# Linear attention with an FFN on one core: the row maxima of K as bias of the exponentials, v in bf16 and unscaled, a new order of the work

## The chip, the cores and the metric

The kernel runs on one core of one Trainium2 chip. Its time is that of one execution on the device, in microseconds (us). Five engines work side by side, each through its own instructions in order: TensorE (PE, the matrix products, with a separate row for loading its weights, PEld), VectorE (DVE), ScalarE (ACT), GpSimd (POOL) and SyncE (SP). PE writes its products into eight banks of 128 x 512 floats; DVE and ACT read the banks. DMAs are issued by SP, by POOL (those that convert a type on the way) or by ACT.

## The reference

Eight batches of eight heads, 576 rows of 64 numbers, go through a linear attention with exponential features; the heads are joined and go through a gated FFN of width 1536.

```python
def phi(x):
    proj = np.einsum('bhsd,df->bhsf', x, w_phi)             # 64 -> 128
    proj = proj - np.max(np.abs(proj), axis=-1, keepdims=True)
    return np.concatenate([np.exp(proj), np.exp(-proj)], axis=-1)
q_p, k_p = (phi(q), phi(k))
kv = np.einsum('bhsf,bhsd->bhfd', k_p, v)
z = np.sum(k_p, axis=2)
num = np.einsum('bhsf,bhfd->bhsd', q_p, kv)
den = np.einsum('bhsf,bhf->bhs', q_p, z)[..., None] + 1e-06
x = num / den                                             # then (b s) (h d)
out = (np.maximum(x @ w_gate, 0) * (x @ w_val)) @ w_out
```

With m the row maximum of |proj|, the two halves of a row's features are exp(proj) e^-m and exp(-proj) e^m.

## The kernel before, in words

**Order.** The text ORDER at the top of the file is the program: each word names a step, its indices and, behind the colon, the banks it uses. The last loop of the file calls the steps in that order, and each engine, POOL's and SP's queues of DMAs among them, gets its instructions in this order. No scheduler changes it. A step waits only for the data and the buffers that it needs.

**Tiling.** Of the 576 rows of a batch the first 512 are four tiles of 128; the last 64 of two batches are joined to tiles of a ninth group, "mix". The eight heads are in three groups (`HEADS`: 0-1, 2-4, 5-7; index j). Index i is one of the four tiles.

**K side.** `lk` loads and converts k (POOL). `kt` (DVE), or in batch 0 `k0` and `k1` (PE and DVE), transposes it; `kr` (L476), in batch 0 `k2` (L514), projects it, rows on the partitions, three heads of 128 features in one bank. `ke` (L523) takes exp(proj) and exp(-proj), index s, of 384 columns at a time, and `kx` (L531) the row maxima of |proj|. The factors e^-m and e^m are not put on the features: `kk` (L540) and `kp` (L551) take them as small exponentials of 12 columns, and `vs`, `vo` and `vr` on POOL (L578, L590, L597), in batch 0 also `vd` and `vp` on DVE, multiply v by them, into two scaled copies of v with a column of the factors. `kv` (L618) then adds up five products for each head and sign: four tiles and the joined rest. `kc` or `kd` copies the sums from the bank on ACT or DVE.

**Q side.** `lq` loads q, `qt` transposes it (L645), `qc` and `qs` project it (L654), features on the partitions; `qe` (L669) takes both exponentials of 512 columns, `qx`, `qy`, `qz`, `qu` find the row maxima, `qw` the factor e^2m. `nu` (L717) multiplies with kv, `nt` and `nv` (L738, L748) join the two signs, `nr` and `nx` (POOL, L760) or `ny` (DVE) divide. `xt` (L777) transposes the result x by a DMA on SP's queue; two tiles of batch 0 go by PE instead (`xp`, L782) and a copy by DVE (`xc`, L790).

**FFN.** For batch 0, `pv` and `pg` (L891) start a third of the width for one tile of 128 rows at a time ("half-FFN" in the prediction stands for the first of these steps); for all else `fv` and `fg` (L865) take 128 of the 1536 columns for 512 rows, `va` (ACT, L880) copies the value half, `ga` (DVE, L883) joins it with the gate. `fo` (L920) multiplies with w_out, `oc` (ACT, L929) copies the result and `od` sends it. `mc` to `mn` are the same as the Q side for the mix group.

**Loads.** v comes in float32: batch 0 by POOL's queue in rows of four, the others by SP's queue (`lv`, `lw`) in rows of 64 floats. k, q, v have one buffer each, so that a batch's load waits for the last reader of the batch before; `gt` is a tiny DMA that keeps the load of batch 1's k behind batch 0's. The weights come by POOL's queue in thirds (`wl`, `wo`). `zz` steps are products of zeros that keep PE's clock up while it waits (L373).

Of the kernel before, what the change touches and what calls it, by code (L numbers as in the profile page):

```python
# [16 lines left out]
ms.0 ms.6 wq ms.2 ms.5 wd ms.4 lk.0.1 ms.3 lq.0.1 lk.0.2 id if zz.22:0 k0.1:0 k1.1:0 zz.5:1  # L17
k2.1:1234 ke.0.1.0.0:1 lk.0.0 lm.0.0 qt.0.1 ke.0.1.2.1:3 lm.0.1 kx.0.1.1:2 zz.3:5 k0.2:5
ke.0.1.2.0:3 kx.0.1.0:1 ke.0.1.3.1:4 k1.2:5 ke.0.1.0.1:1 zz.4:6 k2.2:6705 kx.0.1.2:3 wp
ke.0.1.1.0:2 k0.0:1 kx.0.1.3:4 ke.0.1.1.1:2 kx.0.2.1:7 ke.0.2.0.0:6 k1.0:1 ke.0.1.3.0:4  # L20
ke.0.2.3.0:5 kx.0.2.0:6 ke.0.2.1.0:7 kx.0.2.2:0 kk.0.1.0 zz.4:3 k2.0:3241 wc ke.0.2.1.1:7
kx.0.0.2:4 ke.0.0.3.1:1 kk.0.1.1 qs.0.1.0:7 ke.0.0.3.0:1 lv.0.1 lq.0.0 ke.0.2.2.1:0 kx.0.2.3:5
kp.0.2.1:5 ke.0.0.2.1:4 lv.0.0 kx.0.0.1:2 kx.0.0.3:1 qe.0.1.0.1:7 ke.0.2.3.1:5 ke.0.2.2.0:0 qt.0.0
qs.0.0.0:1 lm.1.1 qx.0.1.0:7 ke.0.0.2.0:4 kp.0.2.0:5 ke.0.0.1.0:2 gt.0 ke.0.2.0.1:6 lv.0.2 lw.0.0
lw.0.1 wl.1.0 kx.0.0.0:3 lk.1.3 vd.0.2.0:5 vo.1 lv.1.2 qs.0.1.1:0 wl.0.0 qs.0.0.2:4 ke.0.0.1.1:2
vs.0.1.0 qs.0.0.1:6 vs.0.1.1 kk.0.0.1 vr.0.0.1 qe.0.0.0.1:1 vr.0.1.1 vd.0.2.1:5 qe.0.0.0.0:1
qx.0.0.2:4 qx.0.0.0:1 qe.0.1.0.0:7 kk.0.0.0 vr.0.1.0 qe.0.1.1.0:0 qx.0.0.1:6 qs.0.0.3:2
ke.0.0.0.0:3 qs.0.1.3:7 vr.0.0.0 lw.1.1 vp.2:5 qe.0.0.3.1:2 qx.0.1.1:0 ke.0.0.0.1:3 qs.0.1.2:1
qy.0.0:5 qz.0.0:5 qe.0.0.1.1:6 kv.0.2:3 qx.0.0.3:2 kv.0.1:5 qe.0.1.3.0:7 qu.0.0 qe.0.0.1.0:6
qe.0.1.1.1:0 qx.0.1.2:1 kc.0.2:3 qw.0.0 kc.0.1:5 qx.0.1.3:7 wl.0.1 vs.0.0.1 qy.0.1:6 qz.0.1:6  # L30
kt.1.1 nu.0.0.2:0 vs.0.0.0 nt.0.0.2:0 qe.0.1.2.1:1 vo.0 kv.0.0:3 qe.0.1.2.0:1 kc.0.0:3
qe.0.0.3.0:2 qu.0.1 nv.0.0.2:0 qy.0.2:6 qz.0.2:6 qw.0.1 nu.0.0.1:5 nt.0.0.1:5 qe.0.1.3.1:7
qe.0.0.2.1:4 nu.0.1.1:1 nu.0.0.0:0 qu.0.2 qw.0.2 nv.0.0.1:5 qy.0.3:3 qz.0.3:3 nu.0.1.0:6 zz.2:2
kr.1.1:2537 nt.0.0.0:0 lm.1.0 nt.0.1.0:6 qe.0.0.2.0:4 nv.0.0.0:0 nt.0.1.1:1 ke.1.1.2.0:3 lq.1.2
wl.1.1 nu.0.1.2:0 nr.0.0 nu.0.2.2:4 nv.0.1.1:1 ny.0.0 nt.0.1.2:0 ke.1.1.1.0:5 nv.0.1.0:6
ke.1.1.3.0:7 ke.1.1.0.0:2 ke.1.1.1.1:5 lw.1.0 nv.0.1.2:0 zz.2:1 xp.0.0:1 wl.0.2 xc.0.0:1
nt.0.2.2:4 nr.0.1 nx.0.1 ke.1.1.2.1:3 nu.0.2.0:6 nu.0.2.1:0 qu.0.3 qw.0.3 nt.0.2.0:6 ke.1.1.3.1:7
nv.0.2.2:4 nv.0.2.0:6 ke.1.1.0.1:2 nt.0.2.1:0 pg.0.0:1 kx.1.1.1:5 nv.0.2.1:0 kx.1.1.2:3 pv.0.0:4
xp.0.1:6 nr.0.2 nx.0.2 xc.0.1:6 xt.0.2 pv.1.0:5 nu.0.3.0:0 pa.0.0:4 pb.0.0:1 pa.1.0:5 ln.0.1
pv.0.1:3 pa.0.1:3 lv.1.0 qt.1.1 kx.1.1.3:7 pg.0.1:4 nt.0.3.0:0 kx.1.1.0:2 kk.1.1.0 nv.0.3.0:0  # L40
pb.0.1:4 nu.0.3.1:6 qc.1.1:1537 qe.1.1.0.0:1 nu.0.3.2:2 qe.1.1.0.1:1 nt.0.3.1:6 qe.1.1.1.0:5
nt.0.3.2:2 qe.1.1.3.0:7 nv.0.3.1:6 pv.1.1:0 lv.1.3 nv.0.3.2:2 pg.1.1:4 pa.1.1:0 lv.1.1 nr.0.3
qx.1.1.0:1 qe.1.1.2.0:3 ln.0.0 qe.1.1.1.1:5 qx.1.1.3:7 qe.1.1.3.1:7 pg.1.0:6 pv.0.2:2 nx.0.3 ku.1
pa.0.2:2 xt.0.3 qe.1.1.2.1:3 pg.0.2:1 pb.1.0:6 kt.1.0 kr.1.0:0672 ke.1.0.1.0:6 wo.2 qx.1.1.1:5
wl.1.2 ke.1.0.3.1:2 pb.1.1:4 qx.1.1.2:3 ke.1.0.0.0:0 ke.1.0.2.1:7 ms.1 ke.1.0.2.0:7 kx.1.0.1:6
ke.1.0.1.1:6 pv.1.2:5 lm.2.0 lm.2.1 pb.0.2:1 pa.1.2:5 vs.1.1.0 wo.0 ke.1.0.0.1:0 pg.1.2:4
kx.1.0.3:2 ke.1.0.3.0:2 qt.1.0 fv.0.9:3 kk.1.1.1 kx.1.0.0:0 fv.0.8:1 pv.0.3:6 va.0.9:3 pb.1.2:4
qc.1.0:5203 vs.1.1.1 va.0.8:1 pa.0.3:6 kt.1.2 qx.1.0.1:2 kx.1.0.2:7 qe.1.0.3.0:3 qx.1.0.3:3 lk.2.3
wo.1 pv.1.3:4 qe.1.0.0.0:5 qx.1.0.0:5 qe.1.0.1.0:2 kk.1.0.0 vr.1.1.0 vs.1.0.0 vr.1.0.0
qe.1.0.1.1:2 kk.1.0.1 vo.1.0 vs.1.0.1 qe.1.0.3.1:3 pg.0.3:1 pb.0.3:1 vr.1.1.1 qe.1.0.0.1:5  # L50
pg.1.3:6 vr.1.0.1 qx.1.0.2:0 pa.1.3:4 mt.0 lv.2.3 pb.1.3:6 qe.1.0.2.0:0 fv.0.10:7 kr.1.2:2315
kx.1.2.1:3 fg.0.10:4 ke.1.2.3.1:5 kx.1.2.0:2 fv.0.11:6 qe.1.0.2.1:0 qy.1.0:0 va.0.10:7 kx.1.2.2:1
kx.1.2.3:5 ke.1.2.1.0:3 vo.1.1 qz.1.0:0 qu.1.0 va.0.11:6 ga.0.10:4 fg.0.11:7 ga.0.11:7 kk.1.2.1
vs.1.2.1 kk.1.2.0 ke.1.2.0.0:2 ke.1.2.3.0:5 fg.0.8:6 ga.0.8:6 kv.1.0:0 ke.1.2.1.1:3 ke.1.2.0.1:2
vs.1.2.0 ku.2 ke.1.2.2.1:1 mc.0:4537 lv.2.0 me.0.3.0:7 mx.0.1:5 mx.0.2:3 vo.1.2 mx.0.0:4
ke.1.2.2.0:1 kt.2.0 fg.0.9:2 ga.0.9:2 lv.2.1 qw.1.0 me.0.3.1:7 me.0.1.0:5 me.0.2.0:3 kv.1.1:6
ln.1.0 kv.1.2:1 kc.1.0:0 mx.0.3:7 lm.3.1 kt.2.1 lq.2.2 ln.1.1 nu.1.1.0:0 kc.1.1:6 nu.1.0.1:2
me.0.1.1:5 nt.1.0.1:2 lv.2.2 me.0.0.0:4 nu.1.0.0:6 nt.1.0.0:6 nv.1.0.1:2 nv.1.0.0:6 nu.1.1.1:7
# [12 lines left out]
oc.0.3:1 lk.3.3 kk.2.1.1 mn.0.1:5 nt.8.0.1:5 mn.0.2:7 vr.2.1.0 vr.2.1.1 kx.2.2.2:0 ke.2.2.2.1:0
nv.8.0.1:5 kk.2.2.1 vr.2.0.1 ke.2.2.0.1:3 lw.3.0 nt.8.0.2:7 nv.8.0.2:7 lm.4.1 fv.1.0:2 va.1.0:2
# [164 lines left out]
def kernel(  # L237
# [94 lines left out]
    def v_in(b):  # L332
        return v_one() if b == 1 else vn_of(b)
# [646 lines left out]
```

## Time and profile before

| | |
|---|---|
| median of 3 runs | 387.66 us (385.79 to 388.32) |
| the profiled execution: span from the first to the last instruction | 384.0 us |
| PE busy | 365.5 us (95%), 3551 products |
| DVE busy | 275.2 us (72%) |
| ACT busy | 237.0 us (62%) |
| POOL busy | 160.1 us (42%) |
| moved by DMA | 38.29 MB, mean 100 GB/s |

The profiled execution has only its span; what lies around it is taken as the 3.7 us between span and median. In the profile a busy PE is not PE at its peak, since products overlap; how far apart they start tells more. The same holds for ACT: its mean durations contain an overlap with the next instruction. "Granted clock" is the share of full speed that the throttle gave to TensorE.

### The profile page before, as it was taken

The page shows a single profiled execution, that of the slowest core. Times are in us where ns is not written, and L with a number is a line of the kernel's source. Part 1 is how long each engine was busy: PE and PEld are TensorE (multiplying, and loading weights), DVE is VectorE, ACT ScalarE, POOL GpSimd, SP SyncE. Part 2 cuts the span into 40 slices and gives each one's busy share as a digit, 9 for nine tenths or more (in the row PEclk, how much of TensorE's full clock was granted, in tenths as well). Part 3 has the DMA queues.
Part 4 walks back from the last instruction along what each step waited for, and adds up shares of the span by engine and source line. Part 5 has one row for each costly group of instructions (what it writes and reads, how often), then busy time and mean ns, then how long its engine had stood idle before and what let it go on. Part 6 is the DMA issues. An engine that isn't in the chain of part 4 may idle for free.

```text
span 384.0 us, 9108 instructions
## 1 busy us (share of the span) xinstructions
PE 365.5 (95%) x3551; PEld 193.7 (50%) x3551; DVE 275.2 (72%) x651; ACT 237.0 (62%) x566; POOL 160.1 (42%) x179
## 2 busy tenths in 40 slices
PE   7699679999999999999999999999999999999994
PEld 4268646545544554455545544464445544444442
DVE  4979929999997898788957797798667822521320
ACT  2987849788867915985787647964977213321321
POOL 8593729587366423672393025811462120100000
PEclk9869979999999999999999999999999999999998
DMA  8999999995965765677335742552410031000114
GB/s 131 231 167 183 181 179 154 131 127 81 215 54 124 114 106 81 122 116 109 77 88 93 134 83 65 111 102 56 112 55 2 3 82 56 27 15 0 55 63 103
DMA packets 91456, 38.29 MB, mean 100 GB/s; under 512 B 65302, under 2 KB 86550, under 8 KB 91414
## 3 DMA queue, kind: packets, MB, share of 16 engines
q0 software_dynamic: 33904, 15.23, 30.6%
q1 hardware_dynamic: 57510, 22.49, 27.4%
q8 instruction: 28, 0.46, 0.5%
q14 instruction: 14, 0.11, 0.1%
HBM read 37.95 MB, written 9.44 MB: 123 GB/s over the span
## 4 chain that ended last, share of the span: by engine, by line
PE 85%; DVE 6%; DMA 4%; SPq 1%; issue 1%; POOL 1%; ACT 0%; DVEq 0%; POOLq 0%
PE bank L865 45%; PE bank L920 25%; PE bank L618 6%; PE bank L717 3%; DMA xTs<-xu 2%; PE bank L654 2%; PE bank L476 2%; DMA qn<-in_q_dram 2%; DVE mk L531 1%; DVE t L738 1%; DVE u L748 1%; PE bank L891 1%; SPq L424 1%; DVE maxq L677 1%; PE bank L852 1%
## 5 line engine op out<-in xcount | busy, mean ns | idle before, releaser
L880 ACT CAST val<-bank 128x512 bf16<-128x512 f32 x100 | 58.0, 599 | 77.3 <-PE bank L865 56.4
L883 DVE SCALAR_TENSOR_TENSOR h<-bank,val 128x512 bf16<-128x512 f32 x100 | 66.7, 678 | 50.3 <-PE bank L865 37.0
L920 PE MATMUL bank<-wo,h 128*128 128x512 bf16 x432 | 99.0, 379 | 0.0
L523 ACT ACTIVATE kp<-bank 128x384 bf16<-128x384 f32 x192 | 81.9, 517 | 20.1 <-PE bank L476 8.3
L865 PE MATMUL bank<-xTs,wv 128*128 128x512 bf16 x352 | 88.2, 384 | 5.9 <-DMA xTs<-xu 5.7
L760 POOL TENSOR_TENSOR xu<-u,r 128x512 bf16<-128x512 f32 x35 | 36.4, 1043 | 124.4 <-DVE r L756 81.7
L865 PE MATMUL bank<-xTs,wg 128*128 128x512 bf16 x352 | 87.9, 379 | 0.0
L669 ACT ACTIVATE qp<-bank 128x512 bf16<-128x512 f32 x128 | 70.7, 627 | 4.4 <-PE bank L654 3.7
L920 PEld LDWEIGHTS <-h 128*128 128x128 bf16 x432 | 40.8, 98 | 47.7 <-issue 0.9
L865 PEld LDWEIGHTS <-wv 128*128 128x128 bf16 x400 | 37.1, 98 | 47.9 <-issue 9.7
L578 POOL TENSOR_TENSOR vs<-vn,ek 128x780 bf16<-128x780 f32 (+3 forms) x40 | 53.0, 1341 | 18.7 <-ACT ek L540 12.2
L865 PEld LDWEIGHTS <-wg 128*128 128x128 bf16 x400 | 36.6, 98 | 42.0 <-issue 3.3
L677 DVE TRANSPOSE_TENSOR_REDUCE maxq<-bank 128x16 f32<-128x512 f32 x64 | 42.4, 692 | 16.8 <-ACT val L906 7.3
L531 DVE TENSOR_REDUCE mk<-bank 128x3 f32<-128x384 f32 x96 | 49.3, 542 | 7.0 <-ACT kp L523 4.6
L929 ACT COPY ob<-bank 128x512 f32<-128x512 f32 x36 | 21.4, 598 | 29.9 <-PE bank L920 26.6
L748 DVE TENSOR_TENSOR u<-bank,t 128x195 f32<-128x195 f32 (+1 forms) x108 | 34.3, 332 | 2.7
L738 DVE TENSOR_TENSOR t<-bank,cq 128x195 f32<-128x195 f32 (+1 forms) x96 | 30.1, 327 | 3.2 <-PE bank L717 2.1
L717 PEld LDWEIGHTS <-qp 128*128 128x128 bf16 x512 | 23.8, 99 | 11.6 <-issue 0.6
L717 PE MATMUL bank<-kv,qp 128*128 128x65 bf16 x512 | 26.4, 195 | 0.2
L597 POOL TENSOR_TENSOR vr<-vm,ek 64x260 bf16<-64x260 f32 x32 | 19.7, 618 | 16.7 <-issue 9.8
L618 PEld LDWEIGHTS <-kp 128*128 128x128 bf16 x640 | 24.1, 102 | 3.3 <-DVE h L883 0.2
L618 PE MATMUL bank<-vs,kp 128*128 128x65 bf16 x512 | 24.3, 199 | 0.0
(81 smaller groups left out, 317.9 us busy)
## 6 DMA issues: line engine op xcount, KB each, us to landing
out_dram<-ob SPq DMA_DIRECT2D x32, 256.0 KB, 2.2
vn<-in_v_dram SPq DMA_DIRECT2D x24, 256.0 KB, 4.6
kn<-in_k_dram POOLq DMA_DIRECT2D x7, 512.0 KB, 8.4
qn<-in_q_dram POOLq DMA_DIRECT2D x7, 512.0 KB, 6.2
wg<-in_moe_w_gate_dram POOLq DMA_DIRECT2D x3, 512.0 KB, 8.4
wv<-in_moe_w_val_dram POOLq DMA_DIRECT2D x3, 512.0 KB, 8.6
wo<-in_moe_w_out_dram POOLq DMA_DIRECT2D x3, 512.0 KB, 13.3
vm<-in_v_dram SPq DMA_DIRECT2D x16, 64.0 KB, 4.1
```

What stands on the lines that cost most here:

```text
L523: nc.scalar.activation(kp_of(3 * b + j)[:, i, s].rearrange("p n f -> p (n f)"), bank[bk[0]][:, 0 : 3 * F], AF.Exp, scale=(1.0, -1.0)[s],)
L531: nc.vector.tensor_reduce(mk_of(3 * b + j)[:, :, i], bank[bk[0]][:, 0 : 3 * F].rearrange("p (n f) -> p n f", f=F), axis=AX.X, op=ALU.max, ...
L578: nc.gpsimd.tensor_tensor(vs_of(3 * b + j)[:, s, 0:n].rearrange("p n i e -> p (n i) e")[:, :, 0:e], src[:, lo:hi].rearrange("p h i e -> p ...
L618: nc.tensor.matmul(out_ps[:, h - lo, s, :], lhsT=lhsT, rhs=rhs, start=(at == 0), stop=(at == 2 * n * (C + 1) - 1),)
L669: nc.scalar.activation(qp_of(4 * b + i)[:, s, 4 * hq : 4 * hq + 4].rearrange("p h m -> p (h m)"), bank[bk[0]], AF.Exp, scale=(1.0, -1.0)[s],)
L677: nc.vector.tensor_reduce(maxq[:, :, i, 4 * hq : 4 * hq + 4].rearrange("p t h -> p h t"), bank[bk[0]].rearrange("p (h t u) -> p h t u", h= ...
L717: nc.tensor.matmul(bank[bk[0]][:, E * n : E * (n + 1)], lhsT=qp_of(4 * b + i)[:, s, h, :], rhs=kv_of(b)[:, h, s, :],)
L748: nc.vector.tensor_tensor(u_of(serial(b, i))[:, lo:hi], parts(bk, n)[:, :, 0], t_of(3 * serial(b, i) + g)[:, 0:n], op=ALU.add,)
L865: nc.tensor.matmul(bank[bk[0]], lhsT=w[:, dc, P * f : P * f + P], rhs=xT(g)[:, dc, :], start=(dc == 0), stop=(dc == NDC - 1),)
L880: nc.scalar.copy(val_of(NFC * g + f), bank[bk[0]])
L883: nc.vector.scalar_tensor_tensor(h2_of(g, f), bank[bk[0]], 0.0, val_of(NFC * g + f), op0=ALU.max, op1=ALU.mult)
L920: nc.tensor.matmul(bank[bk[0]], lhsT=h2_of(g, f)[:, P * t : P * t + P], rhs=wo_sb[:, f, :], start=(f == 0), stop=(f == NFC - 1),)
```

## The change

- `ke` takes one head, 128 columns, at a time, with m or -m as the bias of the exponential, a value per partition read from memory. `kx` writes m, and `kg` (POOL) or `kh` (DVE) writes -m beside it. So the features are scaled, and `kk`, `kp`, `vs`, `vo`, `vr`, `vd`, `vp` are gone.
- v is converted to bf16 by its DMA and goes into `kv` as it is, with a column of ones. All of its loads are on POOL's queue now, in rows of 64, batch 0 too. `gt` is gone; k, q and v have two buffers.
- All four tiles of batch 0's x are transposed by PE (`xp`), with copies by ACT (`xa`, three) or DVE (`xc`, one).
- 36 of the 100 `va` are `vb`, on DVE; 13 of the 36 `oc` are `oe`, on DVE; 17 of the 24 copies of kv are on ACT, 6 before; 8 of the 36 divisions are on DVE, 1 before.
- The last tile is copied in halves by ACT and DVE (`o1`, `o2`), and sent by two DMAs, on SP's and on ACT's queue.
- ORDER is new throughout. Words now also name the buffers (behind @). It begins with 37 zero products in place of 22; the mix group's FFN comes ahead of the last of batch 7's.

```diff
-ms.0 ms.6 wq ms.2 ms.5 wd ms.4 lk.0.1 ms.3 lq.0.1 lk.0.2 id if zz.22:0 k0.1:0 k1.1:0 zz.5:1
+ms.0 ms.1 ms.3 ms.4 ms.2 ms.6 wq wd lk.0.1 ms.8 id zz.37:0 k0.1:0 k1.1:0@kT0 zz.5:1 k2.1:0123 lk.0.2
 ...
-    vn_of = ring("vn", 1, [P, H, C, E], FP32)
+    vn_of = pair("vn", [P, H, C, EP], BF16)
 ...
     def do_lv(bk, b, i):
         if b == 0:
-            lo, hi = HEADS[i]
-            nc.gpsimd.dma_start(
-                out=v_flat()[:, lo:hi],
-                in_=v[b, lo:hi, 0:SF, :].rearrange("h (p c) d -> p h c d", c=C),
-            )
+            src = v[b, :, 0:SF, :].rearrange("h (p c) d -> p h c d", c=C)[:, :, i, :]
         else:
-            nc.sync.dma_start(
-                out=v_in(b)[:, :, i, 0:D],
-                in_=v[b, :, P * i : P * i + P, :].rearrange("h p d -> p h d"),
-            )
+            src = v[b, :, P * i : P * i + P, :].rearrange("h p d -> p h d")
+        nc.gpsimd.dma_start(out=vn_of(b)[:, :, i, 0:D], in_=src)
 ...
     def do_ke(bk, b, j, i, s):
-        nc.scalar.activation(
-            kp_of(3 * b + j)[:, i, s].rearrange("p n f -> p (n f)"),
-            bank[bk[0]][:, 0 : 3 * F],
-            AF.Exp,
-            scale=(1.0, -1.0)[s],
-        )
+        for n in range(3):
+            nc.scalar.activation(
+                kp_of(3 * b + j)[:, i, s, n],
+                bank[bk[0]][:, F * n : F * (n + 1)],
+                AF.Exp,
+                bias=mk_of(3 * b + j)[:, s, i, n : n + 1],
+                scale=(1.0, -1.0)[s],
+            )
 ...
+    def negate(eng, b, j, i):
+        mk = mk_of(3 * b + j)
+        eng.tensor_scalar(mk[:, 0, i], mk[:, 1, i], -1.0, None, op0=ALU.mult)
 ...
     def do_kv(bk, b, j):
 ...
-                        rhs = vs_of(3 * b + j)[:, s, h - lo, i, :]
+                        rhs = vn_of(b)[:, h, i, 0:E]
 ...
-                        rhs = vr_of(b)[:, s, h // 2, h % 2, :]
+                        rhs = vr_of(b)[:, h // 2, h % 2, :]
 ...
+    def do_xa(bk, b, i):
+        nc.scalar.copy(
 ...
+    def do_vb(bk, g, f):
+        nc.vector.tensor_copy(val_of(NFC * g + f), bank[bk[0]])
 ...
+    def do_o1(bk, g, t):
+        nc.scalar.copy(ob_of(4 * g + t)[:, 0:HD], bank[bk[0]][:, 0:HD])
+    def do_o2(bk, g, t):
+        nc.vector.tensor_copy(ob_of(4 * g + t)[:, HD:DM], bank[bk[0]][:, HD:DM])
+    def do_d1(bk, g, t):
+        r0 = S * g + P * t
+        nc.sync.dma_start(out=out[r0 : r0 + P, 0:HD], in_=ob_of(4 * g + t)[:, 0:HD])
+    def do_d2(bk, g, t):
+        r0 = S * g + P * t
+        nc.scalar.dma_start(out=out[r0 : r0 + P, HD:DM], in_=ob_of(4 * g + t)[:, HD:DM])
```

More of the change, by code (lines that the diff above doesn't have):

```diff
@@ L23 @@
[L23 to L34, printed above, removed]
@@ L356, in do_if, with ones @@
         nc.vector.tensor_copy(identf, ident)
+    def ones(b):
+        for hh in range(2):
+            r = slice(SM * hh, SM * (hh + 1))
+            nc.vector.memset(vr_of(b)[r, :, hh, D : D + 1], 1.0)
     def do_ms(bk, what):
@@ L790, in do_xc @@
         nc.vector.tensor_copy(
+            xT_cols(b, i),
+            bank[bk[0]].bitcast(BF16)[:, 0 : NDC * P].rearrange("p (a b) -> p a b", b=P),
+        )
+    def do_xa(bk, b, i):
+        nc.scalar.copy(
             xT_cols(b, i),
```

577 lines of the change are left out of this document (290 added, 287 removed).

## The prediction

> **What bounds the kernel now.** I read the busy tenths first, then the table by stage, then PE's waits and PE in order of time, and last ACT's bursts.
>
> From the page, the busy tenths of PE and ACT and the granted clock in 40 slices:
>
> ```profile
> PE   7699679999999999999999999999999999999994
> ...
> ACT  2987849788867915985787647964977213321321
> ...
> PEclk9869979999999999999999999999999999999998
> ```
>
> PE is full from the seventh slice to the last but one. The table by stage (us of the stage, busy us and instructions of PE, weight loads, DVE, ACT, POOL, then granted clock, DMA share, GB/s):
>
> ```profile
> 8.00:32.00 24.00, 18.09 (x243) 11.35 (x238) 21.59 (x53) 21.63 (x58) 15.87 (x21) 0.79 1.22 200
> ...
> 44.00:60.00 16.00, 10.34 (x124) 6.36 (x122) 8.66 (x16) 8.96 (x23) 7.94 (x10) 0.79 1.29 181
> 60.00:120.00 60.00, 60.00 (x705) 31.83 (x704) 57.53 (x146) 47.76 (x123) 40.63 (x47) 1.00 0.92 123
> ...
> 300.00:384.00 84.00, 79.12 (x431) 36.60 (x427) 27.20 (x63) 21.21 (x39) 5.18 (x5) 0.98 0.16 46
> ```
>
> After 60 us PE is full at clock 1.00, and its instructions follow each other at one step each (four 128x512 matmuls start 0.86 us apart). So the time is: PE's own work, plus what PE loses in the head, plus the tail. By start-to-start steps PE's work is 344 us: 800 matmuls of L865 and 432 of L920 at 0.216 (266), 256 of L891 at 0.0555 (14), 640 of L618 and 512 of L717 at 0.032 (37), the rest (projections, transposes, L852) 27. The last matmul ends at 379.1, so **35 us are lost** in the head (zero matmuls, waits, clock 0.5); the tail is 4.9 us (copy of the last tile 0.59, then its DMA). The span of 384.0 is 3.7 below the median of the runs, 387.66; I add 3.7 to every span.
>
> The largest single loss, in PE's waits and in PE's instructions in order of time (start, us, what):
>
> ```profile
> PE bank L865 <- DMA xTs<-xu: 5.7, 1, 5.7
> ...
> 43.59 1.06 PE L891 MATMUL bank<-xTs,wg 128*128 128x128 bf16 x16
> 50.31 3.50 PE L865 MATMUL bank<-xTs,wv 128*128 128x512 bf16 x8 [5.66 <-DMA xTs<-xu]
> ```
>
> PE waits for x tiles 2 and 3 of batch 0, which go by a DMA transpose behind a full set of loads, and the eight matmuls that follow take 0.43 each in place of 0.216, at half clock: 5.9 + 1.7 = 7.6 us.
>
> **Part by part.**
>
> *x of batch 0 by TensorE.* Two more tiles of four transposes: 8 x 0.056 = 0.45 us of PE, and copies of 0.40 to 0.48 on ACT or DVE. It takes away the 7.6 us, if nothing else is late there. What is late next is ACT's queue, below.
>
> *128-wide exponentials with a bias.* The costly groups (line, engine, operation, count, busy us, mean ns):
>
> ```profile
> L523 ACT ACTIVATE kp<-bank 128x384 bf16<-128x384 f32 x192 | 81.9, 517 | 20.1 <-PE bank L476 8.3
> L578 POOL TENSOR_TENSOR vs<-vn,ek 128x780 bf16<-128x780 f32 (+3 forms) x40 | 53.0, 1341 | 18.7 <-ACT ek L540 12.2
> L597 POOL TENSOR_TENSOR vr<-vm,ek 64x260 bf16<-64x260 f32 x32 | 19.7, 618 | 16.7 <-issue 9.8
> ```
>
> A mean duration overstates ACT, since instructions overlap. ACT in order of time:
>
> ```profile
> 10.38 2.79 ACT L523 ACTIVATE kp<-bank 128x384 bf16<-128x384 f32 x7 [0.46 <-DVE mk L531]
> 12.99 0.27 ACT L540 ACTIVATE ek<-mk 128x12 f32<-128x12 f32 x1
> 13.09 0.93 ACT L523 ACTIVATE kp<-bank 128x384 bf16<-128x384 f32 x2
> 13.84 0.28 ACT L540 ACTIVATE ek<-mk 128x12 f32<-128x12 f32 x1
> 13.94 0.94 ACT L523 ACTIVATE kp<-bank 128x384 bf16<-128x384 f32 x2
> ...
> 27.93 1.12 ACT L669 ACTIVATE qp<-bank 128x512 bf16<-128x512 f32 x2
> 28.89 0.26 ACT L710 ACTIVATE cq<-mz 128x8 f32<-128x8 f32 x1
> ```
>
> Start to start, a 384-wide exponential takes 0.371 (seven from 10.38 to 12.99), a 512-wide one 0.478, and a 12-wide one that reads SBUF 0.10 (13.84 to 13.94). From the first two: 0.833 ns an element and 0.051 us beside; the 12-wide one has 0.092 beside. So a 128-wide exponential from PSUM costs 0.051 + 0.107 = 0.158 if its bias costs nothing, and 0.158 + 0.092 = 0.25 if fetching the row maximum from SBUF costs as much as that read does. Call it p. No row shows an exponential with a bias from memory. I take **p = 0.17**, near the lower end: function, source and destination are those of the 384-wide row, and in the bursts each start lies 0.11 to 0.29 us ahead of the end before it, room enough for a fetch of 0.09. Both ends stay for the range.
>
> By the Trainium skill (ScalarE: Activation LUTs, What ACT_TABLE_LOAD costs) "each `[128,1]` pointer operand adds ≈ 93 ns", and instructions in a row overlap by about 93 ns; before has immediate biases only, so no run here shows it yet. If the 93 ns also stand between two starts, an exponential would take 0.158 + 0.093 = 0.25, the upper end above, and the sum would be that of the second case below.
>
> 192 x 0.371 = 71 us of ACT become 576p: 98 at 0.17, 144 at 0.25. 48 small exponentials (5 us), 36 copies of the value half and 13 output copies (23) leave ACT, 11 copies of kv (4) come. All ACT: 217 before, 220 after (p = 0.17) or 267. DVE takes 36 copies (about 0.60 each, by L629's 260 and 390 wide, 0.41 and 0.55, less the overlap of 0.08) and 13 output copies: 256 to 289 of some 375. POOL loses 82 us (L578, L597, L590) and gains 48 loads of v at 0.75 and 67 negations at about 0.25 (L590 has 0.29 for 24 columns): 157 to some 125. Over the whole span no engine passes PE; what counts is the order in the head.
>
> *The head, on ACT.* PE begins with 37 zero matmuls in place of 22: these 22 end at 5.7 (0.20 each), 15 more at the later 0.109 reach 7.4, and K's first transposes start there in place of 6.6. The first exponential now also needs its row maximum (0.54): 8.3 + 0.8 + 0.6 = 9.7. Up to the first half-FFN of batch 0 ACT has 78 exponentials and 8.8 us of others in its queue; before had 21.5 us and 2.0 us of idle to that point (31.8). So this step comes at 9.7 + 2.0 + 8.8 + 78p = 33.8 for p = 0.17, with 8.8 us of PE's work done: **25 us lost**. At the first gate step over all four tiles (fg.0.10) 131 exponentials and 21.2 us of others lie ahead: 11.7 + 21.2 + 22.3 = 55.2, less 29.2 of PE's work, 26. From there ACT falls behind PE no more at this p: at kv.3.0 (288 exponentials, 46.6 others, PE 90.4) it would allow 17. DVE, by its rows, has 41.8 us ahead of fg.0.10, after 8.5 of early idle, and 29 small negations at 0.1: 52, so it is nearly as late. I add 2.5 for the small waits between the half-FFN and 60 us, of which before has about 4: **28.5 lost**.
>
> *v as bf16, unscaled.* On the path this spares the wait for POOL's scaling (before, DVE scales one group itself, two times 0.94). Its DMAs leave SP's queue for POOL's. All 36,864 rows of v become packets of 128 bytes; such packets took 32 ns in the trace, the present 256-byte ones 23: the v of batches 0 and 1 takes 18.7 us of all 16 DMA engines in place of 11.3, at a share of about 1.25 some 6 us more, behind which the weights lie. Against it, POOL no longer stands 4.2 us for a marker load and k has two buffers. I let these cancel: wo's last third lands near 63 as now, and PE wants its first third at 37.1 + 28.5 = 65.6. So hidden, by a little; this cover gone costs what the load is late.
>
> *Last tile in halves.* The copy goes from 0.59 to about 0.40 (a 256-wide one has 0.41), with two DMAs side by side: 0.4 us off the tail, bounds 0 and 1.
>
> Sum: PE's work with the transposes 344.7, + 28.5 + 4.5 = 377.7 of span, with 3.7 a time of 381; at p = 0.158 the same steps give 1.5 less. I say **380**.
>
> **Rivals.**
> 1. *The bias is paid between two starts (p = 0.25).* Then ACT's queue is the bound for three batches: lost at kv.3.0 are 11.7 + 46.6 + 72 - 90.4 = 40, at the half-FFN 31. Span 344.7 + 40 + 1.5 of waits + 4.5 = 390.7, time **394.5**, slower. It decides from the p at which these losses equal the present 35: about 0.23. For it speaks that the read of SBUF does stand between starts in the 12-wide row (0.092 against 0.051); against it, the starts ahead of ends. Chance 0.25.
> 2. *The loads hold the head.* If the DMA engines keep a share of 1.0 on small packets in place of 1.25, wo is some 7 us late, the loss is 35 as now: **387**. For it: a DMA share of 1.2 to 1.3 all through the head. The Trainium skill (DMA: Bandwidth & Descriptors, Specifications) wants 512 bytes a transfer for full rate; the trace agrees, 512-byte packets taking 64 ns and 128-byte ones 32. Chance 0.10.
> 3. *Small waits eat it.* A negation on POOL stands behind a normalisation (1.04) or a load's issue (0.75) while ACT, in order, waits for it; or p is 0.20, with 30 + 2.5 lost. Either gives **384 to 386**. Chance 0.10.
> 4. The forecast: 375 to 385, chance 0.55.
>
> **Numbers.** One per cent is about what a measurement of this kernel can tell from no change; its edges are 383.8 and 391.5. Faster by more: 0.47 of the forecast, 0.03 and 0.04 of rivals 2 and 3, 0.54. Within: 0.06, 0.05, 0.04, 0.01: 0.16. Slower: 0.24 of rival 1 and 0.06 of the rest: 0.30. The range runs from 374 (p = 0.158, no small waits) to 395.5, which takes in most of rival 1; beyond it lie p near 0.3 and a part of the best cases. The likeliest case's own range is 375 to 385.
>
> **What would show it.** In the changed profile: the start-to-start of the 128-wide exponentials (0.16 to 0.19, or 0.25); no wait of L865's successor for xTs in batch 0; the half-FFN's first matmul near 34 (40 in rival 1); PE full from about 60 on, with ACT at nine tenths to some 55 us only (to 130 in rival 1); PE waiting for a DMA of wo or v in rival 2; ACT waiting for mk from POOL in rival 3. I am wrong if PE still shows idle slices after 65 us, or if DVE, whose 57.53 of 60 us between 60 and 120 leaves least room, becomes what PE waits for.

## The result, and the profile after

The changed kernel takes **443.31 us** (median of 4, 442.99 to 443.63) where the kernel before takes 386.73 (median of 4, 383.21 to 388.32): a ratio of **1.147**, 95% interval 1.141 to 1.152. Forecast was 380.0, with a range up to 395.5. The profiled execution has a span of 441.9 us, 57.9 more than before.

The busy tenths of PE and ACT and the granted clock in 40 slices, from the page of the changed kernel:

```profile
PE   8468888879888699788987999789878999999996
...
ACT  2989999699887656887798635896698630210110
PEclk9759999999999899999999999999999999999999
```

Before, PE stood at nine from the seventh slice on. Now it shows eights and sevens among them as far as the thirty-first slice, some 340 us: the loss is not in the head alone. The table by stage of the changed kernel (stage, its length, then busy us and instructions of PE, weight loads, DVE, ACT, POOL, granted clock, DMA share, GB/s):

```profile
0.00:60.00 60.00, 43.73 (x561) 30.77 (x563) 41.57 (x109) 49.20 (x157) 34.51 (x57) 0.86 1.05 122
60.00:120.00 60.00, 50.50 (x617) 28.34 (x623) 48.38 (x113) 52.69 (x170) 27.91 (x49) 1.00 0.94 107
120.00:180.00 60.00, 51.28 (x479) 26.21 (x485) 47.20 (x114) 40.23 (x120) 20.97 (x33) 0.97 0.58 70
180.00:240.00 60.00, 50.81 (x484) 25.49 (x490) 47.49 (x109) 49.49 (x156) 21.47 (x34) 1.00 0.89 96
240.00:300.00 60.00, 53.16 (x533) 26.99 (x538) 45.32 (x103) 41.95 (x128) 12.79 (x20) 1.00 0.38 52
300.00:360.00 60.00, 52.73 (x462) 26.29 (x471) 43.48 (x98) 43.34 (x126) 5.24 (x11) 1.00 0.17 42
```

From 60 to 360 us PE is busy 258.5 of 300 us; each stage of 60 loses 7 to 10. Before it was busy 299.8 of 300, and the stage in which it was least full was this one:

```profile
120.00:180.00 60.00, 59.77 (x617) 31.24 (x616) 49.83 (x119) 40.78 (x98) 28.93 (x29) 1.00 0.68 112
```

In those 300 us of the changed kernel ACT is busy 227.7 and DVE 231.9: neither is full, not even the engine for whose exponentials PE waits. The chain that ended last, by engine and by line (L543 is the exponential of K, L855 and L916 the FFN):

```profile
PE 42%; ACT 36%; DVE 15%; issue 4%; DMA 2%; POOL 1%; DVEq 0%; ACTq 0%; POOLq 0%
ACT kp L543 25%; PE bank L855 24%; PE bank L916 8%; ACT qp L635 6%; DVE maxq L643 4%; DVE mk L552 3%; DVE h L876 3%; PE bank L584 2%; PE bank L683 2%; DMA xTs<-xu 2%; PE bank L620 2%; PE bank L490 2%; ACT val L870 2%; PE bank L401 1%; DVE u L714 1%
```

Before, ACT had none of this chain:

```profile
PE 85%; DVE 6%; DMA 4%; SPq 1%; issue 1%; POOL 1%; ACT 0%; DVEq 0%; POOLq 0%
```

And PE's waits in the changed kernel (what waits, for whom, us in total, times, longest):

```profile
PE bank L620 <- ACT kp L543: 6.7, 9, 1.6
PE bank L916 <- ACT kp L543: 6.6, 6, 2.0
PE bank L490 <- ACT kp L543: 4.5, 6, 1.3
PE bank L683 <- ACT kp L543: 3.8, 8, 1.2
PE bank L855 <- ACT kp L543: 3.5, 8, 0.9
...
PE bank L855 <- DMA xTs<-xu: 1.9, 1, 1.9
```

Many waits of about one us, at every kind of product. All rows of this list add up to 53 us, and those that end with an exponential of K to 31 of them; before, all rows were 13 us. The one long wait of before (5.7 us for xTs in batch 0) is gone; the 1.9 us for xTs here come at 239 us, in a later batch.

What an exponential costs is read from ACT in order of time (start, us, what, count, idle before). First the changed kernel, then the experiment n128_no_bias below, which differs only in having no bias. Each row begins with the first exponential of K:

```profile
9.50 6.83 ACT L543 ACTIVATE kp<-bank,mk 128x128 bf16<-128x128 f32 x26 [7.50 <-DVE mk L552]
```

```profile
9.15 7.25 ACT L543 ACTIVATE kp<-bank 128x128 bf16<-128x128 f32 x42 [7.14 <-DVE mk L551]
```

In about the same time 26 and 42 instructions. Start to start it is **0.250 us** with the bias (the median of 518 pairs) and **0.158** without (518 pairs too).

### The profile page after: what moved, and what is told of

It is laid out like the page before. It is cut to its first block, busy times and chain, and to the rows that moved or that the text cites. A ratio compares the mean times of both kernels' runs of the same rounds, so it can differ in the third digit from the quotient of the medians.

```text
span 441.9 us, 9415 instructions
## 1 busy us (share of the span) xinstructions
PE 379.5 (86%) x3526; PEld 199.8 (45%) x3575; DVE 316.0 (72%) x726; ACT 286.7 (65%) x867; POOL 123.9 (28%) x201
## 4 chain that ended last, share of the span: by engine, by line
PE 42%; ACT 36%; DVE 15%; issue 4%; DMA 2%; POOL 1%; DVEq 0%; ACTq 0%; POOLq 0%
ACT kp L543 25%; PE bank L855 24%; PE bank L916 8%; ACT qp L635 6%; DVE maxq L643 4%; DVE mk L552 3%; DVE h L876 3%; PE bank L584 2%; PE bank L683 2%; DMA xTs<-xu 2%; PE bank L620 2%; PE bank L490 2%; ACT val L870 2%; PE bank L401 1%; DVE u L714 1%
## 5 line engine op out<-in xcount | busy, mean ns | idle before, releaser
L543 ACT ACTIVATE kp<-bank,mk 128x128 bf16<-128x128 f32 x576 | 160.4, 500 | 26.7 <-DVE mk L552 19.8
L916 PE MATMUL bank<-wo,h 128*128 128x512 bf16 x418 | 99.7, 379 | 7.9 <-ACT kp L543 6.6
L855 PE MATMUL bank<-xTs,wv 128*128 128x512 bf16 x335 | 87.2, 381 | 9.9 <-ACT kp L543 2.3
L855 PE MATMUL bank<-xTs,wg 128*128 128x512 bf16 x336 | 86.0, 379 | 2.8 <-ACT kp L543 1.2
L635 ACT ACTIVATE qp<-bank 128x512 bf16<-128x512 f32 x128 | 72.6, 675 | 12.0 <-DVE maxq L643 6.8
L870 ACT CAST val<-bank 128x512 bf16<-128x512 f32 x64 | 39.7, 625 | 51.1 <-PE bank L855 32.9
L916 PEld LDWEIGHTS <-h 128*128 128x128 bf16 x432 | 40.6, 98 | 53.8 <-issue 9.0
L855 PEld LDWEIGHTS <-wv 128*128 128x128 bf16 x400 | 37.3, 98 | 51.3 <-issue 14.2
L552 DVE TENSOR_REDUCE mk<-bank 128x3 f32<-128x384 f32 x96 | 49.2, 545 | 14.6 <-PE bank L490 12.1
L739 POOL TENSOR_TENSOR xu<-u,r 128x512 bf16<-128x512 f32 x28 | 29.2, 1043 | 107.8 <-DVE r L735 93.1
L855 PEld LDWEIGHTS <-wg 128*128 128x128 bf16 x400 | 37.0, 98 | 45.0 <-issue 7.8
L562 POOL TENSOR_SCALAR mk<-mk 128x3 f32<-128x3 f32 x67 | 15.3, 234 | 119.0 <-DVE mk L552 106.3
L925 ACT COPY ob<-bank 128x512 f32<-128x512 f32 x22 | 14.6, 663 | 41.8 <-PE bank L916 41.0
L873 DVE CAST val<-bank 128x512 bf16<-128x512 f32 x36 | 24.4, 683 | 13.8 <-PE bank L855 13.5
L683 PE MATMUL bank<-kv,qp 128*128 128x65 bf16 x512 | 28.1, 194 | 5.6 <-ACT kp L543 3.8
L445 POOL DMA_DIRECT2D vn<-in_v_dram x32 | 29.5, 923 | 1.5 <-issue 0.7
```

The costliest lines, as they stand in the source:

```text
L543: nc.scalar.activation(kp_of(3 * b + j)[:, i, s, n], bank[bk[0]][:, F * n : F * (n + 1)], AF.Exp, bias=mk_of(3 * b + j)[:, s, i, n : n + 1 ...
L552: nc.vector.tensor_reduce(mk_of(3 * b + j)[:, 1, i], bank[bk[0]][:, 0 : 3 * F].rearrange("p (n f) -> p n f", f=F), axis=AX.X, op=ALU.max, ...
L635: nc.scalar.activation(qp_of(4 * b + i)[:, s, 4 * hq : 4 * hq + 4].rearrange("p h m -> p (h m)"), bank[bk[0]], AF.Exp, scale=(1.0, -1.0)[s],)
L683: nc.tensor.matmul(bank[bk[0]][:, E * n : E * (n + 1)], lhsT=qp_of(4 * b + i)[:, s, h, :], rhs=kv_of(b)[:, h, s, :],)
L855: nc.tensor.matmul(bank[bk[0]], lhsT=w[:, dc, P * f : P * f + P], rhs=xT(g)[:, dc, :], start=(dc == 0), stop=(dc == NDC - 1),)
L870: nc.scalar.copy(val_of(NFC * g + f), bank[bk[0]])
```

## The experiments

Each kernel has one profile and one time, beside the kernel before on the same chip; the two with an interval were timed more often. The kernel before took 385.4 us beside the first four that follow, 382.1 beside v_bf16_max_first, n384_exp_first, old_order_biased and before_v_on_pool, 385.5 (median of five) beside the three with new banks, and 386.3 (median of 11, 384.0 to 388.4) beside the others. Kernels of different groups are compared below as they stand; single times of the kernel before lie up to 6 us apart, so a difference of a few us between two groups says little. An edit shifts the lines of a kernel, so the same step has another line number in each.

### The price of the exponential, in the new order

**n128_no_bias**: the bias goes.

```diff
-                bias=mk_of(3 * b + j)[:, s, i, n : n + 1],
```

> The changed kernel, its 576 exponentials of K 128 wide but with an immediate zero as bias; the factors from the row maxima are left out of the features, so the result is that of unscaled K features. Starts of these exponentials should come 0.158 us apart, 0.25 in the changed kernel. Theory A (the fetch of the bias stands between two starts, and each batch pays what it adds, because the order and the few buffers keep ACT from working ahead): ACT gets back 576 x 0.092 = 53 us and the time falls by most of it, to 380 to 393. Theory B (as in rival 1 of the prediction, ACT's price counts only up to batch 3, 14 us, and the rest of the 443 comes from the loads of v, DVE's larger share or the new order): about 428. Theory C (it is not the price but ACT waiting for the maxima and negations, which goes here too): 380 to 393 as well; the run with a constant bias tells A from C.

Measured: **410.0**, 33.3 less than the changed kernel, between theory B and the others. PE's waits for the exponentials of K come to 3.5 us in all, where the changed kernel has 31.

**n384_no_bias** also puts the three pieces together again, as before the change:

```diff
-        for n in range(3):
-            nc.scalar.activation(kp_of(3 * b + j)[:, i, s, n], bank[bk[0]][:, F * n : F * (n + 1)],
-                AF.Exp, bias=..., scale=(1.0, -1.0)[s])
+        nc.scalar.activation(kp_of(3 * b + j)[:, i, s].rearrange("p n f -> p (n f)"),
+            bank[bk[0]][:, 0 : 3 * F], AF.Exp, scale=(1.0, -1.0)[s])
```

> The changed kernel with the old exponential: one of 384 columns, no bias, 0.371 us; the factors are left out as before. Against the run 128 wide without bias this gives the price of the split alone, 192 x 0.10 = 20 us of ACT. Theory A: 370 to 382, 5 to 15 below the run 128 wide, if ACT is still what is late there, the same if DVE or PE is. Theory B: about 425. Below 380 it would also say that the new order itself, with x of batch 0 by TensorE, is worth having.

Measured: **405.5**, which neither theory had. **n128_const_bias** fetches a bias, but from a column of zeros that was written at the start:

```diff
-                bias=mk_of(3 * b + j)[:, s, i, n : n + 1],
+                bias=zcol,
```

> The changed kernel with the bias fetched from a constant column of zeros in memory, so that the exponentials no longer wait for row maxima or negations, which are still computed; the factors are left out. Theory A (price of the fetch): starts 0.25 us apart and 435 to 443. Theory C (waits for the maxima): 380 to 395. Theory B: 440.

Measured: **443.5**, the time of the changed kernel. What the bias carries costs nothing more, nor does the wait for the negations, which goes here (6.9 us of ACT in the changed kernel). The wait for the maxima does not go, other than the expectation says: ACT still has 24.9 us of idle time that ends with a reduction, and the kernel without a bias has 28.6.

```profile
L544 ACT ACTIVATE kp<-bank,zcol 128x128 bf16<-128x128 f32 x576 | 160.1, 502 | 24.9 <-DVE mk L553 24.9
```

(A row of the costliest groups: count, busy us, mean ns, idle before, and what ended most of it.) So between these two kernels only the fetch differs, and its price is clean: 443.5 - 410.0 = **33.5 us** of time for 576 x 0.092 = 53 us of ACT. What the wait for the maxima costs, these runs don't tell; it comes below. The split in three costs ACT 576 x 0.158 - 192 x 0.371 = 20 us, the time 4.5.

Is it a queue that is late once, in the head, as rival 1 had it, or does each batch pay? **bias_in_3_to_7** has the old exponential in the batches 0 to 2.

```diff
     def do_ke(bk, b, j, i, s):
+        if b < 3:
+            (one exponential of 384, no bias)
+        else:
```

> The changed kernel with the 384-wide exponentials without bias in batches 0 to 2 (factors left out there) and the 128-wide with bias in batches 3 to 7. Theory A (each batch pays on its own): five eighths of the loss stay, so if the run 384 wide throughout takes 378, this takes about 378 + 5/8 x 65 = 419. Theory B (only ACT's lag up to batch 3 counts, later batches have room): at most 5 us above the run 384 wide throughout, 383.

Measured: **426.2**, 20.8 above the kernel with the wide exponential throughout (405.5), of 37.8 for all eight batches. Five batches of eight would have 23.6 if each paid alike. The queue that is late once would give 5 at most: it falls.

### What is left of the new order

With the old exponential the new order still takes 405.5, 20 more than the kernel before beside it. Its table by stage has PE short by 3 to 5 us of 60 as far as 300 us:

```profile
60.00:120.00 60.00, 56.81 (x682) 30.01 (x681) 54.63 (x138) 40.98 (x96) 34.84 (x60) 1.00 0.98 112
120.00:180.00 60.00, 55.09 (x546) 27.81 (x544) 50.45 (x113) 37.51 (x84) 19.72 (x30) 1.00 0.72 98
180.00:240.00 60.00, 56.47 (x542) 28.42 (x539) 50.81 (x122) 32.99 (x74) 16.46 (x23) 1.00 0.61 60
240.00:300.00 60.00, 56.40 (x541) 27.62 (x539) 50.24 (x119) 38.39 (x86) 13.85 (x25) 1.00 0.39 74
```

**n384_dve_back**: on top of n384_no_bias, 36 `vb` become `va`, 13 `oe` become `oc`, 8 `ny` become `nx`, and all `kg` and `kh` go. Two places of the order, as they change:

```diff
-ga.4.8:2@hs6 ke.6.0.2.0:1 ga.4.11:4@hs8 kx.6.0.3:0 ke.6.0.3.1:0 kg.6.0.3 ke.6.0.0.1:5
-nu.5.2.2:4 ny.5.0@xu1 xt.5.0
+ga.4.8:2@hs6 ke.6.0.2.0:1 ga.4.11:4@hs8 kx.6.0.3:0 ke.6.0.3.1:0 ke.6.0.0.1:5
+nu.5.2.2:4 nx.5.0@xu1 xt.5.0
```

> The changed kernel with the old exponential (one of 384, no bias: left out is the scaling by the maxima, so the output is another), and on top of it the evictions of val and ob and the normalisations that the new order puts on DVE (36, 13 and 8) given back to ACT and POOL, and the 96 negations left out. The kernel without these returns took 405.5 us, before 385.4. Theory D (the 20 us are work that came to DVE, about 45 us of it, some 18 of them ahead of 300 us): 386 to 392. Theory O (the order itself, which releases banks and buffers too late or too early, whoever evicts): 400 to 407.

Measured: **412.2**, not less but 6.7 more, above both theories. As far as one such change can tell, DVE's larger load isn't it. The waits of ACT in this kernel have a line that is odd (n384_no_bias has it too, with 34.6 us):

```profile
ACT kp L530 <- DVE mk L538: 30.6, 25, 7.5
```

The exponential uses nothing of the maxima here, and still it waits for them. Both read the same bank, and the wait is on a semaphore: the second reader of a bank is made to wait for the first. When the reductions read another tile (n384_max_elsewhere, below), the line is gone.

**before_v_bf16**: the kernel before in its own order, with v in bf16 by POOL's queue and unscaled.

```diff
-                        rhs = vs_of(3 * b + j)[:, s, h - lo, i, :]
+                        rhs = vn_of(b)[:, h, i, 0:E]
 ...
-            nc.sync.dma_start(
-                out=v_in(b)[:, :, i, 0:D],
+        nc.gpsimd.dma_start(out=vn_of(b)[:, :, i, 0:D], in_=src)
```

> The kernel before, in its own order, with v cast to bf16 on loading by POOL's queue and used unscaled, in the new buffers of two; exponentials of 384 without bias, so the scaling by the maxima is left out and the output is another. It takes 64 multiplications and more off POOL, 48 small exponentials off ACT. Theory V (the 20 us that remain in the new order come from v's loads in bf16, 32 of some 0.92 us of POOL each and 71000 packets on that queue): 395 to 405. Theory O or D (they come from the new order or from what it puts on DVE): 378 to 387.

Measured: **392.0**, 5.7 more than before, though POOL is busy 115.6 us in place of 160.1: between the two expectations. **before_v_on_pool** asks why, with only the queue changed:

```diff
-            nc.sync.dma_start(
+            nc.gpsimd.dma_start(
                 out=v_in(b)[:, :, i, 0:D],
```

> The kernel before with nothing changed but the queue of v's loads: those of batches 1 to 7, fp32 as before, are issued by POOL in place of SP. It asks where the 5.7 us of v in bf16 in the old order come from. If from POOL's queue, in which loads stand behind others and behind waits: 389 to 394. If from the cast on the way (packets of 128 bytes to the chip, 71000 in place of 34000 on that queue): 384 to 388.

Measured: **391.9** (before, beside it, 382.1). v in float32 on POOL's queue loses no less than v in bf16, so issuing the loads by POOL is enough to explain the loss, and the cast isn't needed. Small packets aren't needed either: in this run most of v goes in packets of 4096 bytes (2304 of that size, before 256), where SP's queue had packets of 256. What PE itself waits for then is no load of v:

```profile
PE bank L865 <- DMA xTs<-xu: 3.6, 1, 3.6
PE bank L865 <- DVE mk L531: 2.9, 2, 2.0
```

The DMA transposes of x take longer from their issue to their landing (count, median us), first in the kernel before, then in before_v_on_pool; before_v_bf16 has 4.3 too:

```profile
xTs<-xu SPq DMA_TRANSPOSE x30, 2.5
```

```profile
xTs<-xu SPq DMA_TRANSPOSE x30, 4.3
```

In the changed kernel, whose loads of v are on POOL's queue as well, they take 2.6. So what this queue costs in the old order need not be a part of what the new one lost.

**before_v_bf16_n128_const**: the same kernel, old order, with the 128-wide exponential and the column of zeros as bias.

```diff
-            bank[bk[0]][:, 0 : 3 * F],
+                bank[bk[0]][:, F * n : F * (n + 1)],
                 AF.Exp,
+                bias=zcol,
```

> The same kernel with the exponentials of k 128 wide and a bias fetched from a column of zeros (in the new order such a column gave 443.5 us, as the maxima do). ACT gets 192 times 0.38 us, 73 us. Theory P (each batch pays: what ACT gets is not covered by the slack of other batches, in any order): 415 to 445. Theory N (it is the new order that is bad at covering it; before's order has PE full from 60 to 360 us and room on ACT, 237 of 384 us busy): 385 to 400.

Measured: **431.1**, 39.2 above the kernel with the wide exponential. The new order had 38.0 for the same step. The price of the bias and the split is that of the exponential, not of the order; theory N, that before's order has room for it, falls, and that although there too ACT is busy only 304.2 of 429.4 us:

```profile
PE 378.5 (88%) x3551; PEld 197.6 (46%) x3551; DVE 277.2 (65%) x653; ACT 304.2 (71%) x902; POOL 115.5 (27%) x141
```

So the new order itself is left, some 14 us of it by the difference of 405.5 and 392.0 and 19 if the gain of x by TensorE (below) is added. A bias from the maxima demands that in each bank of K the reduction stands ahead of both exponentials: in the new order in all 96 banks, before in 28 (in 27 between them, in 41 behind). **v_bf16_max_first** puts it first in the old order, each word in the place of another of its own three:

```diff
-k2.1:1234 ke.0.1.0.0:1 lk.0.0 lm.0.0 qt.0.1 ke.0.1.2.1:3 lm.0.1 kx.0.1.1:2 zz.3:5 k0.2:5
+k2.1:1234 kx.0.1.0:1 lk.0.0 lm.0.0 qt.0.1 kx.0.1.2:3 lm.0.1 kx.0.1.1:2 zz.3:5 k0.2:5
```

> The kernel that takes v in bf16, unscaled, in the order of before (391.95 us; 384 wide, no bias, the scaling by the maxima left out), with one thing moved: in every one of the 96 banks of K the reduction to the maxima stands ahead of the two exponentials that read the same bank, as a bias from the maxima demands. Before has it first in 28 banks, between the two in 27, last in 41; each word takes the place of another of its own three. In the traces ACT's exponential waits for DVE's reduction of the same bank even where it uses nothing of it (30.6 us, 25 times, in the kernel with the old exponential in the new order), so the second reader of a bank queues behind the first. Theory M (what is left of the new order's 14 to 20 us is that demand): 401 to 410. Theory R (it is something else in the new order; this costs nothing): 389 to 395.

Measured: **406.5**, 14.6 more than before_v_bf16, as theory M has it; ACT's waits for the maxima went from 3.8 us to 39.6:

```profile
ACT kp L494 <- DVE mk L502: 39.6, 25, 8.2
```

**n384_exp_first** does the reverse in the new order, with the places of before (and the negations behind).

```diff
-kx.0.1.2:2 ke.0.1.2.1:2 k0.2:4 kx.0.1.3:3 ke.0.1.3.1:3 k1.2:4@kT0 zz.12:5
+ke.0.1.2.1:2 ke.0.1.2.0:2 k0.2:4 ke.0.1.3.1:3 kx.0.1.3:3 k1.2:4@kT0 zz.12:5
```

> The same from the other side: the changed kernel with the old exponential (405.5 us, new order), with the place of each reduction among the three readers of its bank as before has it (first in 28, between in 27, last in 41), and the 96 negations behind it. Theory M: 390 to 397. Theory R: 403 to 408.

Measured: **432.4**, 27 more: both theories missed. ACT still waits 29.1 us for reductions, of 34.6, and now the reductions wait 12.5 us for exponentials. So this edit hardly took away the wait that it was made for. It moved some 600 words, and moving words out of their places may cost by itself; the 14.6 us above prove nothing either. **old_order_biased** has the change of the arithmetic complete in the old order, made in this crude way:

```diff
+                bias=mk_of(3 * b + j)[:, s, i, n : n + 1],
 ...
-                        rhs = vs_of(3 * b + j)[:, s, h - lo, i, :]
+                        rhs = vn_of(b)[:, h, i, 0:E]
 ...
+kg.0.1.0  (one word behind each of the 96 kx, which stand first)
```

> The whole change of the arithmetic, with the reference's result, in the order of before: v in bf16 unscaled, maxima first in every bank, a negation on POOL behind each reduction, exponentials 128 wide with the maxima as bias. The new kernel, with its own order, took 443.3. If the parts add up (386.3, +5.7 for v, +13 for maxima first by theory M, +39.2 for split and fetch): 440 to 448. If the new order is of itself the worse one by some 14 us (theory R): 428 to 435.

Measured: **461.2**, 18 slower than the new kernel and above both expectations. The new order is better than the old one with words moved by hand.

The next three move nothing: the reductions read a tile of zeros in place of the bank (the maxima are left out), so that nobody waits on a bank for them.

```diff
-            bank[bk[0]][:, 0 : 3 * F].rearrange("p (n f) -> p n f", f=F),
+            other[:, None, :].to_broadcast([P, 3, F]),
```

> The changed kernel with the old exponential (384 wide, no bias: 405.5 us, new order, every word where it is), and the 96 reductions to maxima read a tile of zeros in SBUF of the same count of elements in place of the bank. The maxima are left out, DVE's work stays, and neither ACT waits for a reduction nor a bank for its release by one. Theory M (the demand of maxima first): 386 to 395. Theory R (anything else in the new order): 401 to 406.

Measured: **411.2**, 5.7 more and above both theories. **v_bf16_max_elsewhere**, the control, has the same edit in the old order.

> The control: the kernel with v in bf16 in the order of before (391.95 us), where ACT waited for a reduction for 3.8 us in all, with the same reading of another tile. Both theories: 386 to 393. If it falls below 385, the waits on banks cost there too, and the first run tells less.

Measured: **384.1**, 7.9 less than with the bank and below what both theories had. **const_bias_max_elsewhere** has it in n128_const_bias.

> The changed kernel with the exponentials 128 wide and a bias from a column of zeros (443.5 us, new order), and the reductions reading another tile. Theory M, if it adds to the price of the bias: 426 to 434, as in the order of before with v in bf16 and such a column (431.1). If ACT, fuller by 73 us, hides the wait for the maxima: 438 to 444, and theory R says the same.

Measured: **433.9**, 9.6 less, as theory M has it. With the wide exponential in the new order the wait for the maxima isn't the cause: without it the kernel is 5.7 slower. In the two others the time falls by 8 to 10. This edit takes away more than ACT's wait: in v_bf16 ACT had waited only 3.8 us for reductions, while the reductions had waited 7.9 us for their banks, which goes too. Whether the kernel before would gain as much by it was not run. The losses are not parts of a sum.

Last, the banks. **n384_rebanked**, **after_rebanked** and **v_bf16_rebanked** keep every word in its place and give each product group the free bank to which PE wrote longest ago:

```diff
-vb.3.2:7@val2 fv.3.5:0 ln.3.1 qx.4.0.3:3 qx.4.0.1:4 fo.2.1.0:7 fo.2.1.1:7 qe.4.0.0.1:6@qp1
+vb.3.2:4@val2 fv.3.5:0 ln.3.1 qx.4.0.3:7 qx.4.0.1:3 fo.2.1.0:4 fo.2.1.1:4 qe.4.0.0.1:5@qp1
```

> The changed kernel with the old exponential (384 wide, no bias, the scaling by the maxima left out; 405.5 us), every word in its place, and only the numbers of the banks new: each group of products takes the bank to which PE wrote longest ago among those that are free. Of 207 groups of the FFN and the numerators, 5 in place of 31 then have less than 1.5 us of PE's own work until the next write to their bank, 13 in place of 61 less than 2 us. Theory T (the new order's loss is banks that come back too soon, so that any lateness of ACT or DVE reaches PE): 386 to 396. Theory U (it is the place of the words, whatever the bank): 402 to 410.

> The changed kernel as it is, with the reference's result, and only the same new numbers of banks (443.3 us before them). Theory T: 425 to 434, the price of the bias staying. Theory U: 440 to 446.

> The control: the kernel with v in bf16 in the order of before (391.95 us; 384 wide, no bias), with banks numbered anew by the same rule; 1 group in place of 8 then has less than 1.5 us. Theory T: 386 to 392. Theory U: 389 to 394.

Measured: **441.9** for 405.5, **491.6** for 443.3 (1.277 of before, 1.267 to 1.286), **444.3** for 392.0. All three are 36 to 52 us slower, the reverse of theory T and far from U. Two of PE's waits of after_rebanked; the same two rows have 3.5 and 0.7 us in the changed kernel:

```profile
PE bank L855 <- ACT kp L543: 20.4, 14, 2.9
PE bank L855 <- DVE h L876: 8.5, 9, 2.5
```

The rule was badly chosen, and that is argued from the text of the order, not shown: the bank that PE wrote longest ago is the one that was held longest, so its last reader often stands directly ahead of the next product. In the stretch from 40 to 290 us of PE's own work the order gives a bank to a new product some 360 times. How often does no work of PE stand between the word of the bank's last reader and that of the new product? In the old order 57 times of 362, in the new 80 of 361; with the new numbers 100 and 93. By this count too the new order is the tighter one, but no run changes it alone.

### The first term alone

**before_x0_by_pe**: the kernel before, with the two remaining transposes of batch 0's x by TensorE.

```diff
-xp.0.1:6 nr.0.2 nx.0.2 xc.0.1:6 xt.0.2 pv.1.0:5 nu.0.3.0:0
+xp.0.1:6 nr.0.2 nx.0.2 xc.0.1:6 pv.1.0:5 nu.0.3.0:0
 ...
-nv.0.3.2:2 pg.1.1:4 pa.1.1:0
+nv.0.3.2:2 xp.0.2:2 xc.0.2:2 pg.1.1:4 pa.1.1:0
 ...
-pa.0.2:2 xt.0.3 qe.1.1.2.1:3
+pa.0.2:2 qe.1.1.2.1:3
 ...
-qx.1.1.2:3 ke.1.0.0.0:0
+qx.1.1.2:3 xp.0.3:3 xc.0.3:3 ke.1.0.0.0:0
```

> The kernel before with only the two remaining transposes of x of batch 0 (tiles 2 and 3) moved from the DMA to TensorE and DVE, all else as before, the result the reference's. It removes the two waits of the forecast's first term (5.7 us of PE for xTs, and the like) and adds 8 transposes, 2 evictions. Theory H (that term is worth what the wait of before shows): 378 to 381. Rival (PE is late for its next operand anyway, the head is bound by ACT and DVE): 384 to 386.

Measured: **380.9** (median of 6, 380.3 to 382.1) against 386.3 (median of 11), a ratio of **0.987**, 0.983 to 0.990: a small gain, but clear of zero, and as theory H has it. It is faster than both kernels. The eight products that waited for xTs and then took 3.50 us, at a granted clock of 0.53, in PE's order of time:

```profile
47.01 1.89 PE L865 MATMUL bank<-xTs,wv 128*128 128x512 bf16 x8
```

They start 3.3 us earlier, wait for nothing, and take 1.89, at a granted clock of 1.00.

## Why the prediction was wrong

*The bias: p taken as 0.17.* This step failed first. The argument was that in the bursts "each start lies 0.11 to 0.29 us ahead of the end before it, room enough for a fetch of 0.09". It is no room: with the bias the starts lie at least as far ahead of the ends (0.20 us in the median), and the pitch, the time from start to start, is 0.250. Taking the fetch out gave back 33.5 us. The other bound, 0.158 + 0.092 from the 12-wide row that reads SBUF, was right to the third digit, and so was 0.158 for a piece without a fetch. The Trainium skill (ScalarE: Activation LUTs, What ACT_TABLE_LOAD costs) gives 93 ns for such an operand; the trace agrees (0.092), and shows what that sentence leaves open, that these stand between two starts of a queue that never pauses.

*The sum over the head.* With p = 0.25 the prediction had 394.5 (rival 1), still 49 us short: the right p does not mend the sum. Rival 1's head is right: the first half-FFN was to start near 40 (34 at p = 0.17), and it starts at 39.4:

```profile
39.37 1.05 PE L884 MATMUL bank<-xTs,wv 128*128 128x128 bf16 x16 [0.36 <-ACT xTs L775]
```

What failed is "over the whole span no engine passes PE; what counts is the order in the head", and with it "then ACT's queue is the bound for three batches". This is the step that failed by most. ACT's work was summed from the start as if what it can't do now could be done in a later batch's slack. PE lost 35 us before and was to lose 28.5, or 41.5 in rival 1; by the same count it lost 93 (the last product ends at 437.8, its own work is 344.7). The losses lie in every stage, and bias_in_3_to_7 shows them: the batches 3 to 7 pay 20.8 of 37.8. The sign that the prediction had named for being wrong, idle slices of PE after 65 us, is there. In before's own order, where ACT was busy 60% of the span (233.4 of 390.1 us), the same exponentials cost 39.2. A busy share of 60% or 70% on ACT was no slack here, where the engines take their work in order and hand eight banks to each other.

*The new order itself.* Behind the head the prediction put it at nothing and gave no reason. With the wide exponential it is worth 19 to 25 us, and why stays open.

*x of batch 0 by TensorE.* The mechanism was right and alone it brings 5.4 us; the term was 7.6. In the changed kernel PE has no wait for xTs in batch 0 either; what that brings can't be seen beside the rest.

*v on POOL's queue, "hidden, by a little".* By the runs not hidden: 5.7 us in the old order, which is a small difference of one run. Rival 2 had the size (6 to 7) but another cause, small packets; float32 loads issued by POOL, in packets of 4096 bytes for the most part, lose as much. Whether it is the order of the queue or POOL's time for issuing (POOL is busy 195.3 us in that run, 160.1 before) wasn't separated; nor whether the changed kernel, with its transposes of x as quick as before, pays it at all.

*The last tile in halves.* From the last product's end to the end of the span 4.1 us (441.9 - 437.8), before 4.9: 0.8 saved where 0.4 was the term, inside its bounds.

*The 3.7 us around the span.* A run's time and its own span lie 1.7 to 2.0 us apart in every run (443.63 and 441.9, 385.42 and 383.6). The 3.7 took the span of one execution from the median of three; the term was some 1.9 too large.

*The maxima ahead of the exponentials.* The prediction counted them once, 0.54 at the first exponential, and gave small waits on a negation 4 to 6 us (rival 3). The group of the exponentials (count, busy us, mean ns, idle before and what ended most of it) has 19.8 us of ACT idle behind the reductions of L552; with the reductions on another tile the time fell by 9.6 at this p (const_bias_max_elsewhere). So the term was too small, by about as much:

```profile
L543 ACT ACTIVATE kp<-bank,mk 128x128 bf16<-128x128 f32 x576 | 160.4, 500 | 26.7 <-DVE mk L552 19.8
```

The mean of 500 ns is nearly that of the 384-wide exponential of before (517): a mean duration doesn't show the pitch of 0.250 against 0.371.

The account, as far as the runs carry it: fetch 33.5, split 4.5; x by TensorE -5.4 and v's queue +5.7, both taken from the old order; the rest, 405.5 - 386.3 + 5.4 - 5.7 = **19 us**, lies in the new order and **stays open**; it is 25 if v's queue costs nothing there. In n384_no_bias PE's waits are 25 us in all, 13 before, and no row of them is above 2.3 us: no single product or engine stands out. That it is DVE's load (412.2) or the wait for the maxima (411.2) is excluded as far as one change can exclude it; the banks' numbers can move far more than 19 us, so the choice of banks may be it, or the place of the words. It wasn't separated. Two edits that took away work or waits made n384_no_bias 6 to 7 us slower, so differences below some 8 us between such kernels are not read as causes here; the 4.5 of the split and the 5.7 of v's queue are no more than sizes.

## What to carry to other kernels

A bias per partition from memory added 0.09 us to the pitch of the instructions here, although they overlap; one wide instruction cut in three, so that each has its own bias, pays it three times: 73 us of ACT with the split, in place of 5 us of small exponentials and multiplications on POOL, which was busy 42%. Sum an engine's queue over each stage, not from the start: in this chain of in-order engines that share eight banks, about half of what was added to an engine busy 54% and 60% came through to the time (38.0 and 39.2 of some 73 us). And of a bundle of edits, the one that removes a wait which the profile names can be had alone.

## What the runs showed that was not expected

- The second reader of a bank waits for the first, with no data between them: ACT waited 30.6 us for reductions whose result it did not use. The wait goes when the reductions read another tile, and the order of the words on a bank decides who waits.
- The numbers of the banks alone, with every instruction in its place, are worth 36 to 52 us of some 400.
- Less work can be slower: with 49 copies, 8 divisions and 29 negations taken off DVE n384_no_bias took 6.7 us more, and with no waits on a bank for a reduction 5.7 more. Why, no run shows.
